# Softmax denominators as an extra column of the output matmuls, and a reordered first pooling pass, in a fused attention and max-out kernel

## The chip, the core and the metric

The kernel runs on one core of a Trainium2 chip. The metric is the device time of one execution in microseconds (us), from a handful of repeated runs. The profile is one further execution, recorded by the hardware profiler.

## What is computed

Two steps follow each other. The first is induced-set attention: 32 learned vectors attend to all tokens of a batch and give `h` (32 x 128), and then each token attends to these 32 rows. The second is a max-out feed-forward layer on the result.

```
B, N, m, C = 4, 12544, 32, 128          # d_ff = 1024
def mab(q, kv):
    s = scale * (q @ kv.T);  s = s - s.max(-1)
    a = exp(s);  a /= a.sum(-1) + 1e-09
    return a @ kv
h = mab(I, x)                            # 32 x 128 per batch
y = mab(x, h)                            # 12544 x 128 per batch
g = maximum(y @ w1, y @ w2)
out = g @ w_out
```

The kernel uses max(a, b) = a + max(0, b - a). With E the exponentials of a token's 32 scores and d their sum, the result is

out = (E @ (h w1 w_out) + relu(E @ (h (w2 - w1))) @ w_out) / d.

The first product is called the linear term here. Its small matrix, 32 x 128 per batch, is `m1`; `hwd` is h (w2 - w1), 32 x 1024. The division by d comes last, so only d is needed per token, at the end.

## The kernel before

**Pooling, batch 0.** The tokens of batch 0 arrive by DMA in eight units: five of 16 blocks of 128 tokens, then 2, 8 and 8 blocks. Per unit, `u_transpose` transposes the blocks on TensorE into PSUM and copies them out, half on VectorE and half on ScalarE. `u_scores` multiplies them with the inducing vectors and takes the exponential on ScalarE. `u_accum` sums exponentials (with a matrix of ones) and the weighted tokens on TensorE. The three are staggered: in the round in which unit i is transposed, unit i-1 is scored and unit i-2 accumulated. `u_h` makes `hT4` from the sums. The weights arrive on the same DMA queue; GpSimd makes three quarters of `w21` = w2 - w1 and VectorE one (line 660).

**Main loop.** A batch has 98 blocks of 128 tokens. They are cut into `Block`s of 16 (batch 0 starts with 2, 4 and 8), and each of these into `Part`s of two 128-column groups. The loop runs over a list `seq` of bursts. A burst (lines 452 to 508) issues row-tiled matmuls into four PSUM banks, 128 x 512 each (line 472), optionally opens two final banks with the linear term ("lead", line 487), and empties the four banks with a relu, each on VectorE (line 503) or ScalarE (line 507). A final (lines 520 to 571) takes 16 matmuls with `woutp` (line 543) into one PSUM bank, VectorE multiplies the 128 x 256 result by the reciprocals (line 559), and after two finals a DMA of 256 KB goes out (line 569), from GpSimd's queue for batches 0 to 2 and from SP's for batch 3. There are 196 bursts and 196 finals. Where no lead was made, the final begins with the linear term itself, from the masked copy `m1d` (line 534).

**Denominators.** `dens` runs once for each of the 30 blocks: one matmul of 4 columns for each 128-column group against `ones4` (line 428), into a PSUM bank of its own, and one reciprocal on VectorE for the whole block (line 437).

**The next batch beside it.** While batch b is in the main loop, batch b+1 is pooled at fixed places of `seq`, given by `at`. `p1_scores` and `p1_accum` run on TensorE; GpSimd adds the exponentials up into `eacc` (128 x 16 x 32, line 317). At place 40 `small_fold` sums the 16 slices of `eacc` with one VectorE reduction (line 322); at 42 `small_h` sums over the partitions with a matrix of ones (line 333) and makes `hT4` (lines 336 and 338); at 43 and 44 `small_hwd` and `small_m1` follow.

**What sets the order.** All engines run a fixed order, written out by the program (`manual_schedule`). A small planner, `Model`, keeps a clock for TensorE, VectorE and ScalarE when the program is built; `bank` gives out the PSUM bank that it thinks comes free first, and `pick` gives each relu to the engine that it thinks ends it first. It charges VectorE for extra work through `ev(..., extra)`.

Of the kernel before, what the change touches and what calls it, by code (L numbers as in the profile page):

```python
# [9 lines left out]
F16 = mybir.dt.float16  # L10
F32 = mybir.dt.float32
AF = mybir.ActivationFunctionType
ALU = mybir.AluOpType
ET = mybir.EngineType

# [36 lines left out]
def kernel(  # L52
# [9 lines left out]
    nc = tc.nc  # L62
    B, N, C = x.shape
    M = inducing.shape[0]
# [5 lines left out]
    P1B = 16  # L70
# [8 lines left out]
    NU = len(units)  # L79
# [76 lines left out]
    with tc.manual_schedule(engines={ET.PE, ET.DVE, ET.Activation, ET.Pool, ET.SP}):  # L156
# [26 lines left out]
        def u_transpose(i):  # L183
            t, g0, n = units[i]
            xn = xn_of(0, t)
            step = 4 if i == NU - 1 else 8
            for g in range(g0, g0 + n, step):
                m = min(step, g0 + n - g)
                bi, ps = bank([128, 8, 128], F16)
                end = 0.0  # L190
                for j in range(m):
                    nc.tensor.transpose(ps[:, j, :], xn[:, g + j, :], identity16)  # L192
                    end = model.pe(0.056)
                k = p1_blocks[t][0] + g
                dst = xT_tiles[0][:, k : k + m, :]
                if (g // step) % 2 == 0:
                    nc.vector.tensor_copy(out=dst, in_=ps[:, 0:m, :])  # L197
                    model.bank_free[bi] = model.ev("DVE", 64 * m, end)
                else:
                    nc.scalar.copy(out=dst, in_=ps[:, 0:m, :])  # L200
                    model.bank_free[bi] = model.ev("ACT", 128 * m, end)
# [118 lines left out]
        def small_fold(b):  # L320
            es = smp.tile([128, 1, M], F32, name=f"esum_{b}", tag="esum")
            nc.vector.reduce_sum(  # L322
                out=es[:, 0, :],
                in_=st[b]["eacc"].rearrange("p k m -> p m k"),
                axis=mybir.AxisListType.X,
            )
            model.ev("DVE", P1B * M, 0.0)
            st[b]["esum"] = es[:, 0, :]
# [36 lines left out]
        m1_tiles = [consts.tile([128, C], F16, name=f"m1_{i}") for i in range(2)]  # L365
        m1d_tiles = [consts.tile([128, 4, C], F16, name=f"m1d_{i}") for i in range(2)]
        ones4 = consts.tile([128, 4], F16, name="ones4")
        mask = consts.tile([128, 4, 1], F16, name="mask")

        def small_m1(b):  # L370
# [6 lines left out]
            nc.scalar.copy(out=m1, in_=ps[:, 0:128])  # L377
            model.bank_free[bi] = model.ev("ACT", 128, end)
            nc.gpsimd.tensor_mul(
                m1d,  # L380
                m1[:, None, :].broadcast_to((128, 4, 128)),
                mask.broadcast_to((128, 4, 128)),
            )
# [3 lines left out]
        class Block:  # L387
# [37 lines left out]
            def dens(self):  # L425
                bi, ps = bank([128, 512])
                for tt in range(self.t):
                    nc.tensor.matmul(  # L428
                        out=ps[:, 4 * tt : 4 * (tt + 1)],
                        lhsT=self.e2[:, 128 * tt : 128 * (tt + 1)],  # L430
                        rhs=ones4,
                        start=True,
                        stop=True,
                    )
                    end = model.pe(0.025, max(model.bank_free[bi], self.ready))
                self.rp = rpp.tile([128, self.t, 4, 1], F32, name=f"rp_{self.name}", tag="rp")
                nc.vector.reciprocal(
                    out=self.rp.rearrange("p t q o -> p (t q o)"), in_=ps[:, 0 : 4 * self.t]
                )
                model.bank_free[bi] = model.ev("DVE", 16, end, 0.1)  # L440

        class Part:
# [9 lines left out]
            def burst(self, u, lead=()):  # L452
# [30 lines left out]
                for s in range(2):  # L483
                    for part, q in lead:
# [3 lines left out]
                            out=part.fin[q][1][:, 128 * s : 128 * (s + 1)],  # L488
                            lhsT=part.blk.e2[r, 128 * tt : 128 * (tt + 1)],
                            rhs=st[part.blk.b]["m1"][r, :],  # L490
# [4 lines left out]
                    if lead:  # L495
                        model.pe(0.056, 0.0, "row")
                for q in range(4):
# [22 lines left out]
            def final(self, i):  # L520
# [10 lines left out]
                for s, (q, tt) in enumerate(cols):  # L531
                    o = ps[:, 128 * s : 128 * (s + 1)]
                    if start:
# [3 lines left out]
                            rhs=st[blk.b]["m1d"][:, q, :],  # L537
# [4 lines left out]
                    for jb in range(NJB):  # L542
                        nc.tensor.matmul(  # L543
                            out=o,
# [10 lines left out]
                if self.tn == 2:  # L555
                    rp = blk.rp[:, self.t0 : self.t0 + 2, i, :]
                else:
                    rp = blk.rp[:, 0, 2 * i : 2 * i + 2, :]
                nc.vector.tensor_mul(  # L559
                    self.osb[:, h : h + 2, :],  # L560
                    ps[:, 0:256].rearrange("p (s c) -> p s c", s=2),
                    rp.broadcast_to((128, 2, 128)),
                )
                model.bank_free[bi] = model.ev("DVE", 256, end)
# [38 lines left out]
        nc.vector.tensor_copy(out=ones4, in_=mask.rearrange("p q o -> p (q o)"))  # L603
# [28 lines left out]

        last = NU - 3
        for i in range(last - 1):
            u_transpose(i)
            if i >= 1:
                u_scores(i - 1)
            if i >= 2:
                u_accum(i - 2)
            keep_warm(1)  # L640

        u_transpose(last - 1)
        u_scores(last - 2)
# [4 lines left out]
        u_accum(last - 3)  # L648
# [3 lines left out]
        for i in range(last - 2, NU):  # L652
            u_accum(i)
# [53 lines left out]
        for g, (p, u) in enumerate(seq):  # L707
# [3 lines left out]
            p.burst(u, lead)  # L711
            for blk in stages.get(g, ()):
                blk.stage()
            if g == 0:
                small_m1(0)
# [3 lines left out]
            if u == 0 and p.t0 == 0:  # L719
                p.blk.dens()  # L720
# [38 lines left out]
```

The softmax here doesn't subtract the row's maximum and nothing guards it: scores larger than these inputs give would overflow.

## Time and profile before

| | |
|---|---|
| median of 6 runs | 342.92 us (342.32 to 343.96) |
| the profiled execution's own time | 342.84 us |
| its span in the profile | 341.1 us |
| granted TensorE clock | 1.0 of full speed |
| TensorE busy | 329.4 us (97%) |
| VectorE busy | 298.2 us (87%) |
| ScalarE busy | 270.1 us (79%) |
| GpSimd busy | 87.0 us (26%) |

PE is TensorE, PEld its weight loads, DVE VectorE, ACT ScalarE, POOL GpSimd; L543 is line 543 of the kernel. A group's busy time counts overlapping instructions of an engine once, and a mean is the time of one from start to end, so the two differ where instructions of one engine overlap. The time in brackets in a timeline line is idle time of the engine just before, with what ended it. The 1.7 us between span and time lie outside the recorded instructions.

### The profile page before, as it was taken

The page shows a single profiled execution, that of the slowest core. Times are in us where ns is not written, and L with a number is a line of the kernel's source. Part 1 is how long each engine was busy: PE and PEld are TensorE (multiplying, and loading weights), DVE is VectorE, ACT ScalarE, POOL GpSimd, SP SyncE. Part 2 cuts the span into 40 slices and gives each one's busy share as a digit, 9 for nine tenths or more (in the row PEclk, how much of TensorE's full clock was granted, in tenths as well). Part 3 has the DMA queues.
Part 4 walks back from the last instruction along what each step waited for, and adds up shares of the span by engine and source line. Part 5 has one row for each costly group of instructions (what it writes and reads, how often), then busy time and mean ns, then how long its engine had stood idle before and what let it go on. Part 6 is the DMA issues. An engine that isn't in the chain of part 4 may idle for free.

```text
span 341.1 us, 14479 instructions
## 1 busy us (share of the span) xinstructions
PE 329.4 (97%) x6346; PEld 263.9 (77%) x6346; DVE 298.2 (87%) x622; ACT 270.1 (79%) x523; POOL 87.0 (26%) x148
## 2 busy tenths in 40 slices
PE   8788999999999999999999999999999999999996
PEld 3685688888868878888877887887877787878875
DVE  2247999999899999999998999999998998989994
ACT  1657988777888877887888877787889888889882
POOL 7243111454422233553222131423212100000000
PEclk9999999999999999999999999999999999999999
DMA  7999699589928984995228992212212222222222
GB/s 135 210 270 214 143 263 232 156 171 216 232 83 162 278 192 108 183 249 156 96 93 165 251 209 88 94 65 94 93 67 94 80 96 92 96 95 94 96 96 108
DMA packets 53423, 50.42 MB, mean 148 GB/s; under 512 B 41456, under 2 KB 42128, under 8 KB 53360
## 3 DMA queue, kind: packets, MB, share of 16 engines
q0 software_dynamic: 11408, 33.43, 36.9%
q1 hardware_dynamic: 41952, 16.08, 21.6%
q8 instruction: 49, 0.80, 0.9%
q14 instruction: 14, 0.11, 0.1%
HBM read 27.28 MB, written 25.69 MB: 155 GB/s over the span
## 4 chain that ended last, share of the span: by engine, by line
PE 85%; DMA 4%; DVE 3%; ACT 3%; POOL 2%; issue 2%; POOLq 0%; DVEq 0%
PE ps L543 55%; PE ps L472 18%; DMA xn<-in_x_dram 4%; PE ps L487 4%; ACT relu L507 2%; PE ps L297 2%; PE ps L275 2%; PE ps L407 2%; DVE relu L503 1%; POOL xn L119 1%; DVE o L559 1%; POOL xn L114 1%; DVE esum L322 1%; PE ps L428 1%; PE ps L534 0%
## 5 line engine op out<-in xcount | busy, mean ns | idle before, releaser
L507 ACT ACTIVATE relu<-ps 128x512 f16<-128x512 f32 x445 | 235.8, 602 | 45.4 <-PE ps L472 33.0
L503 DVE TENSOR_SCALAR relu<-ps 128x512 f16<-128x512 f32 x339 | 218.3, 680 | 5.2 <-PE ps L472 4.1
L543 PE MATMUL ps<-woutp,relu 128*128 128x128 f16 x3136 | 209.1, 220 | 0.0
L543 PEld LDWEIGHTS <-relu 128*128 128x128 f16 x3136 | 176.4, 98 | 30.8 <-issue 21.1
L559 DVE TENSOR_TENSOR o<-ps,rp 128x256 f32<-128x256 f32 x196 | 81.9, 418 | 15.4 <-PE ps L543 12.5
L472 PE MATMUL ps<-e,hwd 32*128 32x256 f16 (+1 forms) x1632 | 83.0, 268 | 1.1 <-DVE relu L503 0.3
L569 POOL DMA_DIRECT2D out_dram<-o x75 | 41.0, 547 | 163.6 <-DVE o L559 111.9
L472 PEld LDWEIGHTS <-hwd 32*128 32x128 f16 x1632 | 27.1, 92 | 20.0 <-issue 4.4
L487 PE MATMUL ps<-m,e 32*128 32x128 f16 x372 | 29.8, 214 | 1.2 <-DVE relu L503 0.5
L487 PEld LDWEIGHTS <-e 32*128 32x128 f16 x372 | 18.4, 92 | 7.5 <-issue 4.4
L317 POOL TENSOR_TENSOR eacc<-eacc,et 128x512 f32<-128x512 f32 (+1 forms) x18 | 18.5, 1028 | 0.3
L284 ACT ACTIVATE et<-ps 128x512 f16<-128x512 f32 (+1 forms) x21 | 11.4, 544 | 4.7 <-PE ps L275 4.7
L417 ACT ACTIVATE e<-ps 128x512 f16<-128x512 f32 (+2 forms) x30 | 14.9, 549 | 0.0
L200 ACT COPY xT<-ps 128x1024 f16<-128x1024 f16 (+1 forms) x6 | 5.6, 941 | 11.3 <-PE ps L192 11.3
L114 POOL DMA_DIRECT2D xn<-in_x_dram x21 | 11.5, 550 | 5.3 <-DMA xn<-in_x_dram 4.7
L197 DVE COPY xT<-ps 128x1024 f16<-128x1024 f16 (+2 forms) x8 | 4.9, 608 | 8.3 <-PE ps L192 8.3
L275 PE MATMUL ps<-inducingT,xT 128*128 128x32 f16 x294 | 10.6, 176 | 0.0
L297 PE MATMUL ps<-et,xn 128*128 128x32 f16 x294 | 10.6, 176 | 0.0
L192 PE MATMUL ps<-identity,xn 128*128 128x128 f16 x98 | 6.7, 219 | 3.1 <-DMA xn<-in_x_dram 2.7
L275 PEld LDWEIGHTS <-xT 128*128 128x128 f16 x294 | 9.6, 96 | 0.0
L297 PEld LDWEIGHTS <-xn 128*128 128x128 f16 x294 | 9.5, 96 | 0.0
L407 PE MATMUL ps<-xT,hT 128*32 128x512 f16 (+2 forms) x120 | 8.7, 349 | 0.6 <-DVE w L660 0.4
(65 smaller groups left out, 112.1 us busy)
## 6 DMA issues: line engine op xcount, KB each, us to landing
out_dram<-o POOLq DMA_DIRECT2D x72, 256.0 KB, 3.2
xn<-in_x_dram POOLq DMA_DIRECT2D x23, 512.0 KB, 9.1
out_dram<-o SPq DMA_DIRECT2D x24, 256.0 KB, 2.0
wf<-in_moe_w_dram POOLq DMA_DIRECT2D x2, 512.0 KB, 14.2
xn<-in_x_dram POOLq DMA_DIRECT2D x2, 256.0 KB, 13.7
out_dram<-o POOLq DMA_DIRECT2D x3, 128.0 KB, 5.4
xT<-xn SPq DMA_TRANSPOSE x21, 6.0
xn<-in_x_dram POOLq DMA_DIRECT2D x4, 64.0 KB, 9.3
```

Source lines behind the costliest of these rows:

```text
L114: nc.gpsimd.dma_start(out=xn_of(b, i)[:, 0:n, :], in_=xr[b, :, k0 : k0 + n, :])
L275: nc.tensor.matmul(out=ps[:, j * M : (j + 1) * M], lhsT=xT_tiles[b % 2][:, k0 + j, :], rhs=inducingT, start=True, stop=True,)
L297: nc.tensor.matmul(out=ps[:, 0:M], lhsT=xn[:, j, :], rhs=et[:, j, :], start=(j == 0), stop=(j == n - 1),)
L317: nc.gpsimd.tensor_add(out=acc, in0=acc, in1=et[:, 0:n, :])
L407: nc.tensor.matmul(out=ps[32 * q : 32 * (q + 1), 0 : self.width], lhsT=st[self.b]["hT4"][:, 32 * q : 32 * (q + 1)], rhs=xT[:, q % self.g], ...
L472: nc.tensor.matmul(out=ps[:, jj * w : (jj + 1) * w], lhsT=st[blk.b]["hwd"][r, 128 * jb : 128 * (jb + 1)], rhs=blk.e2[r, 128 * self.t0 : 12 ...
L487: nc.tensor.matmul(out=part.fin[q][1][:, 128 * s : 128 * (s + 1)], lhsT=part.blk.e2[r, 128 * tt : 128 * (tt + 1)], rhs=st[part.blk.b]["m1" ...
L503: nc.vector.tensor_scalar(out=dst, in0=src, scalar1=0.0, scalar2=None, op0=ALU.max)
L507: nc.scalar.activation(out=dst, in_=src, func=AF.Relu)
L543: nc.tensor.matmul(out=o, lhsT=self.relu[:, jb, q, tt, :], rhs=woutp[:, jb, :], start=False, stop=(s == 1 and jb == NJB - 1),)
L559: nc.vector.tensor_mul(self.osb[:, h : h + 2, :], ps[:, 0:256].rearrange("p (s c) -> p s c", s=2), rp.broadcast_to((128, 2, 128)),)
L569: eng.dma_start(out=outr[blk.b, :, k : k + nst, :], in_=self.osb[:, 0:nst, :])
```

## The change

The tiles of `m1` and `m1d` get 132 columns instead of 128, set to 1 beforehand in `m1` and masked in `m1d`. The linear-term matmuls take 129 of them, so the 129th column of each 128-column group of a final's PSUM bank is the denominator. `dens`, `ones4` and their 100 matmuls and 30 reciprocals are gone. Each of the 196 finals has a reciprocal of its own on VectorE, 2 elements wide, just before its multiplication. The planner charges a final 0.16 us more.

Three more places change. `small_fold` runs on GpSimd, as four additions that halve `eacc` (8, 4, 2 and 1 slices of 32), instead of VectorE's reduction. `small_m1(0)` is moved from after the first burst to between that burst's matmuls and its relus, and `m1d` is made in two halves. In the pooling of batch 0, each round transposes unit i, accumulates unit i-1 and then scores unit i; the last three units' copies all go to VectorE, and the last unit is copied in one piece.

```diff
-            step = 4 if i == NU - 1 else 8
+            step = 8
...
-                if (g // step) % 2 == 0:
+                if i >= NU - 3 or (g // step) % 2 == 0:
                     nc.vector.tensor_copy(out=dst, in_=ps[:, 0:m, :])
...
         def small_fold(b):
-            es = smp.tile([128, 1, M], F32, name=f"esum_{b}", tag="esum")
-            nc.vector.reduce_sum(out=es[:, 0, :], in_=st[b]["eacc"]..., axis=X)
-            model.ev("DVE", P1B * M, 0.0)
-            st[b]["esum"] = es[:, 0, :]
+            acc = st[b]["eacc"]
+            n = P1B // 2
+            while n:
+                nc.gpsimd.tensor_add(out=acc[:, 0:n, :], in0=acc[:, 0:n, :], in1=acc[:, n : 2 * n, :])
+                n //= 2
+            st[b]["esum"] = acc[:, 0, :]
...
-            nc.gpsimd.tensor_mul(m1d, m1[:, None, :]..., mask...)
+            for q in (0, 2):
+                nc.gpsimd.tensor_mul(m1d[:, q : q + 2, :], m1[:, None, :]..., mask[:, q : q + 2, :]...)
...
-            def dens(self):
...
-                            out=part.fin[q][1][:, 128 * s : 128 * (s + 1)],
+                            out=part.fin[q][1][:, MS * s : MS * s + C + 1],
-                            rhs=st[part.blk.b]["m1"][r, :],
+                            rhs=st[part.blk.b]["m1"][r, 0 : C + 1],
...
+                pv = ps[:, 0 : 2 * MS].rearrange("p (s c) -> p s c", s=2)
+                rp = rpp.tile([128, 2, 1], F32, name=f"rp_{self.name}_{i}", tag="rp")
+                nc.vector.reciprocal(out=rp, in_=pv[:, :, C : C + 1])
                 nc.vector.tensor_mul(
                     self.osb[:, h : h + 2, :],
-                    ps[:, 0:256].rearrange("p (s c) -> p s c", s=2),
+                    pv[:, :, 0:C],
                     rp.broadcast_to((128, 2, 128)),
                 )
-                model.bank_free[bi] = model.ev("DVE", 256, end)
+                model.bank_free[bi] = model.ev("DVE", 256, end, 0.16)
...
         for i in range(last - 1):
             u_transpose(i)
             if i >= 1:
-                u_scores(i - 1)
-            if i >= 2:
-                u_accum(i - 2)
+                u_accum(i - 1)
+            u_scores(i)
             keep_warm(1)
-
         u_transpose(last - 1)
-        u_scores(last - 2)
+        u_accum(last - 2)
         u_transpose(last)
         u_transpose(last + 1)
         u_scores(last - 1)
         u_transpose(last + 2)
-        u_accum(last - 3)
+        u_accum(last - 1)
         u_scores(last)
         u_scores(last + 1)
         u_scores(last + 2)
-        for i in range(last - 2, NU):
+        for i in range(last, NU):
             u_accum(i)
...
-            p.burst(u, lead)
+            p.burst(u, lead, (lambda: small_m1(0)) if g == 0 else None)
...
-            if g == 0:
-                small_m1(0)
...
-            if u == 0 and p.t0 == 0:
-                p.blk.dens()
```

The order of the changed program differs in one more way, which the diff does not show: with the new charge the planner gives VectorE 305 relus and ScalarE 479, where it gave them 339 and 445.

## The prediction

> **What bounds it now.** I read the chain that ended last first, then the groups by shape, then the engines' busy time in stretches that I cut at the stages, then timelines. Chain and groups:
>
> ```profile
> PE 85%; DMA 4%; DVE 3%; ACT 3%; POOL 2%; issue 2%; POOLq 0%; DVEq 0%
> ```
>
> ```profile
> L428 PE MATMUL ps<-ones,e 128*128 128x4 f16 x100 | 6.8, 165 | 0.0
> L437 DVE RECIPROCAL rp<-ps 128x16 f32<-128x16 f32 x23 | 5.7, 247 | 0.0
> L437 DVE RECIPROCAL rp<-ps 128x4 f32<-128x4 f32 x6 | 1.0, 172 | 0.0
> L317 POOL TENSOR_TENSOR eacc<-eacc,et 128x512 f32<-128x512 f32 x15 | 17.6, 1170 | 0.2
> L317 POOL TENSOR_TENSOR eacc<-eacc,et 128x64 f32<-128x64 f32 x3 | 0.9, 317 | 0.0
> ```
>
> TensorE sets the end, but VectorE runs close behind it. The stretches (length, then busy us of PE, PEld, DVE, ACT, POOL) show how close:
>
> ```profile
> 38.00:96.00 58.00, 57.43 (x1166) 47.58 (x1168) 55.40 (x116) 46.31 (x89) 20.13 (x33) 1.00 0.86 195
> 168.00:190.00 22.00, 21.61 (x396) 16.86 (x388) 20.39 (x42) 19.42 (x41) 4.95 (x10) 1.00 0.60 141
> 246.00:269.00 23.00, 22.62 (x416) 17.56 (x414) 20.97 (x44) 20.43 (x43) 5.30 (x10) 1.00 0.21 83
> 269.00:334.00 65.00, 64.63 (x1212) 51.66 (x1210) 60.81 (x122) 56.92 (x112) 0.54 (x1) 1.00 0.25 94
> ```
>
> So each added VectorE us must find a place in 2 to 7% of idle time, while every TensorE us removed counts where VectorE leaves room. VectorE's true prices are its start-to-start times, in the timeline at the turn from batch 0 to 1:
>
> ```profile
> 92.97 0.32 POOL L317 TENSOR_TENSOR eacc<-eacc,et 128x64 f32<-128x64 f32 x1
> ...
> 93.32 1.04 DVE L322 TENSOR_REDUCE esum<-eacc 128x32 f32<-128x512 f32 x1 [1.10 <-POOL eacc L317]
> ...
> 94.27 0.68 DVE L503 TENSOR_SCALAR relu<-ps 128x512 f16<-128x512 f32 x1
> ...
> 94.87 0.42 DVE L559 TENSOR_TENSOR o<-ps,rp 128x256 f32<-128x256 f32 x1
> ...
> 95.20 0.68 DVE L503 TENSOR_SCALAR relu<-ps 128x512 f16<-128x512 f32 x1
> ...
> 96.13 0.35 DVE L336 RECIPROCAL hrec<-ps 128x32 f32<-128x32 f32 x1
> ...
> 96.51 0.29 DVE L338 TENSOR_TENSOR hT<-hacc,hrec 128x128 f16<-128x128 f32 x1
> ```
>
> A relu holds VectorE for 0.60 us (94.27 to 94.87), a final's multiplication for 0.33 (94.87 to 95.20): successors start before the end. But the multiplication at 96.51, which needs the reciprocal's result, starts 0.38 after it, 0.03 after its end.
>
> **The reciprocals.** Each final gains one, with its multiplication waiting for it on the same engine. By width, 247 ns for 16 columns and 172 for 4 give 6.25 ns a column, so 160 ns for 2; with the 0.03 wait, 0.19 us a final, 196 x 0.19 = 37.2 us. Bounds: 0.09 us (the start-to-start time of a 4-column reciprocal before an independent relu) to 0.38 (the row at 96.13); I take 0.19, since form and dependence are those of that row and only the width is less. Behind the waiting multiplication are queued the next burst's relus, and behind those TensorE's next PSUM banks. Removed from VectorE: 30 block reciprocals at 0.09 to 0.16 (4.6 us), three reductions at 0.87 start to start (2.6), and 339 - 305 = 34 relus at 0.60 (20.4). Net +9.6 us. ScalarE takes the 34 relus at 0.49 (eight in a row last 4.03 us at 169.6; 16.7 us); it has 71 us idle in the span, and this work lies beside TensorE.
>
> [...]
>
> **The matmuls of the denominators.** From a final's first weight load to the next burst's, 4 denominator matmuls between them add little:
>
> ```profile
> 37.95 0.90 PEld L543 LDWEIGHTS <-relu 128*128 128x128 f16 x16
> ...
> 38.81 0.20 PEld L428 LDWEIGHTS <-e 128*128 128x128 f16 x4
> ...
> 39.03 0.12 PEld L472 LDWEIGHTS <-hwd 32*128 32x128 f16 x8
> ...
> 101.86 0.90 PEld L543 LDWEIGHTS <-relu 128*128 128x128 f16 x16 [0.41 <-issue]
> ...
> 102.86 0.23 PEld L472 LDWEIGHTS <-hwd 32*128 32x128 f16 x16
> ```
>
> 1.08 us against 1.00: 0.08 for each of 23 blocks, 1.9 us in all (the small blocks add under 0.1). One PSUM bank more is free meanwhile, which I price at nothing: these stretches show TensorE 98 to 100% busy, so banks are not what it waits for. The 129th column is 1/128 of 392 matmuls that stream 128 columns; at the 63 ns that one of the finals' 16 takes (1.00/16), 392 x 63/128 = 0.2 us; at the least nothing, if weight loads hide it. I take 0.1.
>
> In the stretches 38-96, 112-168 and 190-246, 13 blocks lie; VectorE loses 10, 9 and 10 relus there against 35 or 36 finals, so its load stays within 0.6 us of before. There TensorE's gain is real: 13 x 0.08 = **-1.0**. In the last batch (269-334) I count 44 finals, 72 relus before and 67 after. VectorE's slots go from 72 x 0.60 + 44 x 0.33 + 5 x 0.16 = 58.5 to 67 x 0.60 + 44 x 0.52 = 63.1 us, against 65.0 - 5 x 0.08 = 64.6 that TensorE needs. VectorE would be 98% full in fixed order, and it now loses 4.2 us there idle, mostly waiting for a final's last matmul. I let 0.8 us of stalls reach TensorE: **+0.4** net (0 stalls: -0.4; all of the idle kept: 63.1 + 4.2 = 67.3, so +2.3).
>
> **The fold.** Before, VectorE stood 1.10 us for GpSimd and then 0.95 in the reduction. The finals' starts show what reached TensorE: 93.37 to 96.47 is 3.10 us where a final with lead takes 1.44 and `small_h` 0.35, so 1.3 lost; in the turns at 171 and 249, 1.92 for 1.44, so 0.5 each. After: four GpSimd additions of 256, 128, 64 and 32 elements; the two L317 rows give 0.20 us + 1.9 ns an element, so 0.68, 0.44, 0.32 and 0.26, with gaps of about 0.08 (the setup's GpSimd operations) 2.0 us. In batch 0 it starts when the addition at 92.97 ends and is ready at 95.3, while TensorE wants it at 94.5, where line 333's matmuls start now: 0.8 stall, 0.5 gained. In the others the last `eacc` addition is three places earlier; only GpSimd's output DMA, which waits for a multiplication, stands before the fold (170.19 to 170.75 at batch 1). Ready at 172.8, wanted at 173.4. These turns are VectorE-bound after the change (20 relus remain 20), so I count half of the 0.5s. Sum **-1.0** (bounds -2.3, if the fold is never waited for, to +0.5, if GpSimd's queue makes each turn wait).
>
> **The start.** The first final stands behind `m1d`:
>
> ```profile
> 28.66 1.03 POOL L379 TENSOR_TENSOR m1d<-m,mask 128x512 f16<-128x512 f16 x1 [1.64 <-ACT m L377]
> 29.75 0.22 PE L534 MATMUL ps<-m1d,e 128*128 128x128 f16 x1 [1.18 <-POOL m1d L379]
> ```
>
> With `m1` copied ahead of the first relus and `m1d` in halves (half of 1.03 or a little more), the first half is there before TensorE gets to it: the 1.18 goes. Next is late what the copy delays, two ScalarE relus by its 0.29, and the first finals' multiplications, whose end frees banks for the next burst here, two reciprocals at 0.19. Pooling: a round now waits for the ScalarE copy (1.01 us) of its own unit, so it lasts 1.0 transposes + 1.1 copy's end + 0.3 second half of the scores + 0.2 warming = 2.6 us; four rounds from 7.3 reach 17.8, where the data of the fifth unit came at 17.5. So 0.3 is lost there, but after the last data at 20.2 one accumulation (0.6) less is left. I take 0.35 gained (bounds: 0.6 gained, if the rounds cost nothing; 1.0 lost, if each takes a third of a us longer than worked out). Start: -1.18 - 0.35 + 0.29 + 0.38 = **-0.85**. At the tail one reciprocal lies before the last multiplication: **+0.2**.
>
> **Sum.** -1.0 + 0.4 - 1.0 - 0.85 + 0.1 + 0.2 = -2.15, on the profiled execution's own 342.84 (span 341.1 and 1.74 around it; 0.08 under the median): 340.7 us.
>
> **Rivals.**
> 1. VectorE becomes the bound (slower). In the start, turns and last batch (27-38, 96-112, 168-190, 246-269, 269-334) lie 85 finals: 85 x 0.19 = 16.2, less 6 relus (3.6), 16 block reciprocals (2.6) and 2 reductions (1.7), so +8.3 us. The idle time there is 1.8 + 1.2 + 1.6 + 2.0 + 4.2 = 10.8. If a third of it can be used, 4.7 reach the end; with the gains outside (1.0, batch 0's turn 0.5, the start 0.85) and +0.3: 345.5. It decides when under 60% of that idle time is usable. For it: fixed order, 94% full already. Against: 38-96 ran 96% full with TensorE 99% busy.
> 2. Everything fits (faster still): reciprocals hidden, all 1.9 of the denominators, 2.3 of the folds and 1.5 at the start: 342.84 - 5.7 + 0.3 = 337.4. Against: the slots of the last batch.
> 3. No change: the pooling order costs 1.0 instead of -0.35, and GpSimd's fold stalls TensorE as long as the reduction did (0 instead of -1.0): 340.7 + 2.35 = 343.0.
>
> **How the numbers follow.** My forecast has 0.45, rival 1 0.25, rival 2 0.13, rival 3 0.17. About 0.3% (1 us) is what a measurement of this kernel can tell from no change. Faster takes my forecast, rival 2 and a little of rival 3: 0.60; same 0.15; slower 0.25. The range runs from near rival 2's end to just short of rival 1's: 338.0 to 345.2.
>
> **What would show it.** Right: L428 and L437's 16-column rows gone with nothing new on the chain in 38-96; a 2-column reciprocal near 160 ns with its multiplication 0.19 after its start; no L534 wait at 28; DVE 97% or more busy in the last batch with TensorE spacing near 1.33 and 1.44; a wait of L333 for GpSimd near 0.8 at the first turn only. Wrong: finals in the last batch spaced well over 1.45 on average with waits on VectorE's relus, or a first burst later than 26.6.

## The result, and the profile after

The changed kernel takes 345.73 us (median of 21 executions, 344.21 to 347.83) against 343.52 for the kernel before beside it: ratio 1.0066 [1.0053, 1.0078]. It is slower by 2.2 us, where a gain of 2.15 was forecast, and lies 0.5 us above the top of the range. The profiled execution took 345.81 us, span 344.0; before it was 342.84 and 341.1.

Each execution's mean granted TensorE clock is on record too. It is 0.998 or more in some and 0.993 to 0.995 in most others, and this goes with 1.0 us: the kernel before, over all that follows, has a median of 342.93 us in 37 executions at 0.998 or more and of 343.92 in 51 at 0.993 to 0.995. The last section shows what goes with it in the profiles. The versions have the two in different shares, so beside the medians of all executions I give differences "at full clock": a version's executions at 0.998 or more, against those of the kernel before beside them. The changed kernel is slower by 1.7 us at full clock (344.64, 11 executions) and by 2.0 at the lower one.

I read the same views in the same order. First the chain that ended last, from the page of the changed kernel:

```profile
PE 78%; DMA 6%; issue 6%; ACT 4%; POOL 3%; DVE 2%; POOLq 0%
```

TensorE lost seven points of the chain. "issue", time in which an engine waits for nothing that the profile shows, rose from 2 to 6%; that entry becomes important below. The groups by shape show the new operations as forecast:

```profile
L543 DVE RECIPROCAL rp<-ps 128x2 f32<-128x2 f32 x196 | 32.1, 164 | 10.3 <-PE ps L529 7.8
...
L326 POOL TENSOR_TENSOR eacc<-eacc 128x256 f32<-128x256 f32 x3 | 2.2, 734 | 0.1
L326 POOL TENSOR_TENSOR eacc<-eacc 128x128 f32<-128x128 f32 x3 | 1.4, 453 | 0.2
```

A reciprocal takes 164 ns (160 forecast). The busy time by stretches (length, then busy us of PE, PEld, DVE, ACT, POOL):

```profile
38.00:96.00 58.00, 55.82 (x1116) 45.03 (x1112) 53.29 (x133) 49.11 (x96) 21.58 (x36) 1.00 0.92 195
112.00:168.00 56.00, 55.52 (x1113) 44.67 (x1111) 52.30 (x130) 48.97 (x95) 19.53 (x31) 1.00 0.92 190
168.00:190.00 22.00, 21.70 (x389) 16.59 (x387) 20.88 (x54) 19.96 (x40) 7.32 (x15) 1.00 0.50 122
190.00:246.00 56.00, 55.74 (x1117) 44.76 (x1118) 52.66 (x131) 49.07 (x97) 16.27 (x24) 1.00 0.54 126
246.00:269.00 23.00, 22.69 (x408) 17.30 (x406) 21.87 (x55) 20.47 (x41) 7.14 (x14) 1.00 0.24 89
269.00:337.00 68.00, 67.77 (x1231) 53.54 (x1232) 65.66 (x165) 60.43 (x119) 1.08 (x2) 1.00 0.25 92
```

Only the first row shows a clear loss: TensorE is 96% busy in 38 to 96 where it was 99%. In the other rows it is 99% busy or more, within 1% of before, and yet the same finals take longer, so this view hides part of the loss. The start and the first turn, from the timeline:

```profile
27.71 1.23 POOL L380 TENSOR_TENSOR m1d<-m,mask 128x264 f16<-128x264 f16 x2
...
28.42 0.22 PE L520 MATMUL ps<-m1d,e 128*128 128x129 f16 x1 [0.18 <-POOL m1d L380]
...
94.07 0.42 DVE L544 TENSOR_TENSOR o<-ps,rp 128x256 f32<-128x256 f32 x1
...
94.29 1.98 POOL L326 TENSOR_TENSOR eacc<-eacc 128x256 f32<-128x256 f32 x4
...
96.33 0.41 PE L333 MATMUL ps<-eacc,ones 128*128 128x32 f32 x2 [1.17 <-POOL eacc L326]
```

The wait for `m1d` is 0.18 us instead of 1.18, and the first final starts at 28.47 instead of 29.81. At the first turn TensorE waits 1.17 us for GpSimd's fold; in the other two turns it does not wait.

Where the time went, from the starts of the finals in the two timelines (us, after minus before): up to the first final -1.33; batch 0 (final 1 to 50) +2.14; batch 1 (50 to 99) +0.59; batch 2 (99 to 148) +0.30; batch 3 (148 to 196) +0.73; from the last final to the end of the span +0.54. The sum is +2.97.

What ended TensorE's waits in the loop (the waits view, PE, 36 to 340 us; total, times, longest), for the changed kernel:

```profile
PE ps L333 <- POOL eacc L326: 1.2, 1, 1.2
PE ps L471 <- issue: 1.1, 1, 1.1
PE ps L471 <- DVE relu L489: 0.5, 3, 0.2
PE ps L456 <- issue: 0.5, 1, 0.5
PE ps L471 <- ACT e L418: 0.4, 2, 0.2
PE ps L471 <- ACT relu L493: 0.3, 1, 0.3
```

and the kernel before:

```profile
PE ps L487 <- DVE relu L503: 0.5, 2, 0.3
PE ps L472 <- DVE relu L503: 0.3, 1, 0.3
```

Two waits for the fold and for "issue" stand out, and the lead matmuls (L471) wait more. This view has only a part of it: "issue" apart, it lists 1.2 us at the lead matmuls of the changed kernel and 0.5 at those of the kernel before, while the starts of these matmuls give 2.5 us more (third row below). So I added up the time from each TensorE matmul's start to the next one's start, by kind of step, from the 4th to the 193rd final (my own sum over the trace's records):

| us | before | changed | changed, 2nd profile |
|---|---|---|---|
| whole stretch | 295.91 | 299.62 | 299.10 |
| steps round the denominators, with the turn to the next burst | 22.83 | 20.78 | 20.77 |
| steps within the groups of four lead matmuls, without the next row's | 10.78 | 13.31 | 13.89 |
| stalls without a releaser | 0 | 2.02 | 1.12 |
| final to `small_h` | 0.40 | 1.50 | 1.50 |

The denominators' removal brings its 2.0 us. It is eaten by the leads (+2.5 to 3.1), the stalls without a releaser (+1.1 to 2.0) and the first fold (+1.1). The experiments ask what each of these is.

### The profile page after: what moved, and what is told of

Its sections match the earlier page's. It is cut to its first block, busy times and chain, and to the rows that moved or that the text cites. A ratio compares the mean times of both kernels' runs of the same rounds, so it can differ in the third digit from the quotient of the medians.

```text
span 344.0 us, 14447 instructions
## 1 busy us (share of the span) xinstructions
PE 331.0 (96%) x6246; PEld 260.2 (76%) x6246; DVE 303.3 (88%) x752; ACT 284.6 (83%) x556; POOL 93.2 (27%) x164
## 3 DMA queue, kind: packets, MB, share of 16 engines
q0 software_dynamic: 11408, 33.43, 38.2%
## 4 chain that ended last, share of the span: by engine, by line
PE 78%; DMA 6%; issue 6%; ACT 4%; POOL 3%; DVE 2%; POOLq 0%
PE ps L529 50%; PE ps L456 17%; PE ps L471 4%; DMA wf<-in_moe_w_dram 4%; ACT relu L493 3%; DMA xn<-in_x_dram 2%; PE ps L277 2%; PE ps L299 2%; PE ps L408 2%; DVE relu L489 1%; POOL out_dram L554 1%; POOL xn L116 1%; DVE o L544 1%; ACT e L418 1%; POOL eacc L319 0%
## 5 line engine op out<-in xcount | busy, mean ns | idle before, releaser
L493 ACT ACTIVATE relu<-ps 128x512 f16<-128x512 f32 x479 | 251.5, 606 | 33.4 <-PE ps L456 25.0
L489 DVE TENSOR_SCALAR relu<-ps 128x512 f16<-128x512 f32 x305 | 198.5, 682 | 2.5 <-PE ps L456 1.7
L544 DVE TENSOR_TENSOR o<-ps,rp 128x256 f32<-128x256 f32 x196 | 83.2, 425 | 6.8
L543 DVE RECIPROCAL rp<-ps 128x2 f32<-128x2 f32 x196 | 32.1, 164 | 10.3 <-PE ps L529 7.8
L471 PE MATMUL ps<-m,e 32*128 32x129 f16 x372 | 32.3, 216 | 2.8 <-issue 1.1
L471 PEld LDWEIGHTS <-e 32*128 32x128 f16 x372 | 18.9, 92 | 10.0 <-issue 4.5
L199 DVE COPY xT<-ps 128x1024 f16<-128x1024 f16 (+1 forms) x8 | 5.1, 637 | 8.4 <-PE ps L194 8.4
L202 ACT COPY xT<-ps 128x1024 f16<-128x1024 f16 x5 | 5.1, 1012 | 8.5 <-PE ps L194 8.5
## 6 DMA issues: line engine op xcount, KB each, us to landing
xn<-in_x_dram POOLq DMA_DIRECT2D x2, 256.0 KB, 13.3
```

The lines of the kernel that those rows point to most:

```text
L471: nc.tensor.matmul(out=part.fin[q][1][:, MS * s : MS * s + C + 1], lhsT=part.blk.e2[r, 128 * tt : 128 * (tt + 1)], rhs=st[part.blk.b]["m1" ...
L489: nc.vector.tensor_scalar(out=dst, in0=src, scalar1=0.0, scalar2=None, op0=ALU.max)
L493: nc.scalar.activation(out=dst, in_=src, func=AF.Relu)
L543: nc.vector.reciprocal(out=rp, in_=pv[:, :, C : C + 1])
L544: nc.vector.tensor_mul(self.osb[:, h : h + 2, :], pv[:, :, 0:C], rp.broadcast_to((128, 2, 128)),)
```

## The experiments

### Which part of the change costs

`start_only` is the kernel before with the three edits of the start (pooling order, copies, `small_m1` and the two halves of `m1d`).

```diff
+            u_scores(i)
...
+            p.burst(u, lead, (lambda: small_m1(0)) if g == 0 else None)
```

> Before, with the three changes at the start alone: the new pooling order of batch 0, small_m1(0) ahead of the first relus, m1d in two halves. Theory A (the start gains, the main loop loses): the first final starts 1.3 us earlier, as in the changed kernel, nothing else moves, so 1.0 to 1.5 us faster than before. Rival (the start's gain is given back later, because the next batch's loads set the pace): under 0.4 us faster.

Measured: 341.75 us, ratio 0.9949 [0.9929, 0.9969]: 1.75 us gained, but 0.97 at full clock, which all five of its executions have and only 4 of 16 of the kernel before beside them.

`fold_only` is the kernel before with the fold on GpSimd.

```diff
-            nc.vector.reduce_sum(...)
+            while n:
+                nc.gpsimd.tensor_add(out=acc[:, 0:n, :], in0=acc[:, 0:n, :], in1=acc[:, n : 2 * n, :])
```

> Before, with the fold of eacc on GpSimd alone. Theory A: the three turns no longer lose the 1.3 and twice 0.5 us to VectorE's reduction, but at the first turn TensorE waits about 1.1 us for GpSimd before line 333's matmuls, so 0.5 to 1.5 us faster than before. Rival (the fold on GpSimd is what made the changed kernel slower): 0.5 to 2 us slower.

Measured: 342.51, 0.9966 [0.995, 0.9983]: 1.2 us gained, 0.74 at full clock.

`col_only` is the kernel before with the column, the reciprocals and the planner's charge.

```diff
-            def dens(self):
...
+                nc.vector.reciprocal(out=rp, in_=pv[:, :, C : C + 1])
```

> Before, with the denominators as a 129th column and a reciprocal for each final alone (with the planner's charge); old pooling order, old fold, old place of small_m1. Theory A: this part holds all of the loss. TensorE is rid of 2.1 us of denominator matmuls and waits more than that before the second lead matmul of a final pair, for a bank that ScalarE's third relu of the burst before still empties: 2 to 4.5 us slower than before. Rival (fold or stalls without a named wait made the loss): within 1 us of before.

Measured: 348.72, 1.0156 [1.0135, 1.0178]: 5.4 us lost. It has no execution at full clock; at 0.993 to 0.995 it is 4.9 us slower than the kernel before (348.69 and 343.76). `after_reduce` is the changed kernel with VectorE's reduction put back.

```diff
-                nc.gpsimd.tensor_add(out=acc[:, 0:n, :], in0=acc[:, 0:n, :], in1=acc[:, n : 2 * n, :])
+            nc.vector.reduce_sum(...)
```

> The changed kernel with VectorE's single reduction in place of GpSimd's fold. Theory A: the turns lose what the reduction costs, so 0.5 to 1.5 us slower than the changed kernel (about 3.5 us slower than before). Rival (the fold on GpSimd is what made it slower): 0.5 to 2 us faster than the changed kernel.

Measured: 347.59, 1.0116 [1.0082, 1.015], so the fold gains in the changed kernel too (1.3 us at full clock, 345.98 against 344.64). By the medians the three parts add, -0.51 - 0.34 + 1.56 = +0.71% against 0.66 measured, but that is luck: at equal clock they are -0.97 - 0.74 + 4.9 = +3.2 us, where 1.7 to 2.0 were measured. The column is the only part that loses; how much depends on what stands beside it.

`start_fold` is the change without the column.

> Before, with the three changes at the start and the fold on GpSimd, without the column. If the parts add up, 0.9949 x 0.9966 = 0.9915 of before, about 2.9 us faster; if the fold's gain needs the old start, no more than start_only's 0.5%.

Measured: 341.80, 0.9934 [0.9908, 0.996]: 2.3 us gained of the 2.9 expected. At full clock it is 1.6 (two executions), and there the two parts add (0.97 + 0.74). From here to the changed kernel the column costs 3.3 us at full clock.

### What in the column costs

`after_128` leaves the 129th column out of the matmuls.

```diff
-                            rhs=st[part.blk.b]["m1"][r, 0 : C + 1],
+                            rhs=st[part.blk.b]["m1"][r, 0:C],
```

> The changed kernel with the linear-term matmuls 128 columns wide again (the 129th column is left out, the reciprocals take the last of the 128, so the values are others; every instruction and the order stay). Theory A (the lead matmuls wait for PSUM banks): within 0.5 us of the changed kernel. Rival C (the odd width of 129 columns makes the row-tiled matmuls slower, 93 leads at 0.04 to 0.08 us): 4 to 7 us faster than the changed kernel.

Measured: 345.38, 1.0043 [1.0017, 1.007]. The interval overlaps that of the changed kernel, so the width costs at most about 1 us; at full clock the two are 0.25 us apart (344.39 and 344.64). The profiles show nothing of it: where no bank is late, the starts within a group of leads are 2 to 4, 53 and 3 ns apart at both widths.

`after_norecip` leaves the reciprocals out, in the same order of the relus.

```diff
-                nc.vector.reciprocal(out=rp, in_=pv[:, :, C : C + 1])
+                rp = ones32[:, 0:2].rearrange("p (s o) -> p s o", o=1)
```

> The changed kernel with the 196 reciprocals left out (the multiplications take ones, so the division is left out); the order and the split of the relus, 305 and 479, stay. Theory A1 (what VectorE spends on reciprocals and on waiting for them holds up the banks): 3 to 5 us faster than the changed kernel, about 341 to 342 us. Theory A2 (the planner's new split, three relus of a burst on ScalarE ahead of a lead, holds up the banks): under 1 us faster, the second lead matmul still waits about 0.1 us.

Measured: 342.18, 0.995 [0.9928, 0.9971]. The reciprocals cost 1.16%, some 4 us, and 3.0 at full clock (344.64 to 341.64). `after_nodep` keeps all 196 and only lets the multiplication read ones, so that the division is left out.

```diff
-                    rp.broadcast_to((128, 2, 128)),
+                    ones32[:, 0:2].rearrange("p (s o) -> p s o", o=1).broadcast_to((128, 2, 128)),
```

> The changed kernel with its 196 reciprocals in place, but the multiplications take ones instead of their results, so that none waits for a reciprocal on its own engine (the division is left out). Order and split stay. If the wait counts (0.19 us a final with it, 0.08 to 0.10 without), about half of what leaving the reciprocals out gained comes back: 1.5 to 2.5 us faster than the changed kernel. If a wait between chained VectorE operations costs nothing, no change; if only the wait counts, the whole 3.9 us.

Measured: 342.23, 0.996 [0.9934, 0.9985], the same as without the reciprocals. So 196 more operations on VectorE cost nothing that can be measured here; making the next operation wait for each costs 3.5 us, or 3.0 at full clock, where the ranges lie well apart (341.31 to 342.32 in six executions, 344.21 to 345.82 in the changed kernel's eleven). Its trace was taken once more:

> One profile of the kernel whose multiplications take ones instead of the reciprocals' results, for the waits of its lead matmuls. If the dependent wait makes the leads wait, their sum falls from 9.6 us to about that of the kernel without reciprocals, 6.8; if the time came back elsewhere, it stays near 9.6.

The same final of the last batch in the timeline of the changed kernel

```profile
316.39 1.07 PE L529 MATMUL ps<-woutp,relu 128*128 128x128 f16 x16
316.43 0.16 DVE L543 RECIPROCAL rp<-ps 128x2 f32<-128x2 f32 x1
...
316.63 0.42 DVE L544 TENSOR_TENSOR o<-ps,rp 128x256 f32<-128x256 f32 x1
316.97 0.68 DVE L489 TENSOR_SCALAR relu<-ps 128x512 f16<-128x512 f32 x1
...
317.62 0.35 PE L471 MATMUL ps<-m,e 32*128 32x129 f16 x4
...
317.90 0.51 PE L529 MATMUL ps<-woutp,relu 128*128 128x128 f16 x6
```

and of `after_nodep_look`:

```profile
314.10 0.16 DVE L543 RECIPROCAL rp<-ps 128x2 f32<-128x2 f32 x1
314.16 1.07 PE L529 MATMUL ps<-woutp,relu 128*128 128x128 f16 x16
314.18 0.40 DVE L544 TENSOR_TENSOR o<-ps,ones 128x256 f32<-128x256 f32 x1
...
314.50 0.68 DVE L489 TENSOR_SCALAR relu<-ps 128x512 f16<-128x512 f32 x1
...
315.39 0.29 PE L471 MATMUL ps<-m,e 32*128 32x129 f16 x4
...
315.61 0.56 PE L529 MATMUL ps<-woutp,relu 128*128 128x128 f16 x7
```

From the reciprocal to the relu behind the multiplication it is 0.54 us against 0.40. The four leads then take 0.28 us (317.62 to 317.90) against 0.22, and the next final starts 1.51 us after this one instead of 1.45. The waits that go with the dependence are 60 to 110 ns long, but for one of 33. In the last batch, from the 148th to the 196th final, the independent version takes 67.74 us against 68.73. Over the loop the leads' row falls from 13.3 to 11.9 and the stalls without a releaser from 2.02 to 0.18. So nearly half of the difference is in the leads. More than half is in those stalls, which the last group of runs is about; that the dependence brings them is not shown, and a second profile of the changed kernel has 1.12 us of them beside 13.89 us in the leads.

Is it VectorE's standing still, or the later release of the final's bank? `after_split` puts a relu between the two operations.

```diff
+                    if eng == "DVE" or q == 3:
+                        while pending:
+                            pending.pop(0)()
...
+                pending.append(rest)
```

> The changed kernel with the final's multiplication taken away from its reciprocal: it is issued behind the first relu of the next burst that goes to VectorE (or ahead of the fourth bank's), so that VectorE does independent work while the reciprocal ends. The price is that the final's PSUM bank is held about 0.6 us longer. Theory A (VectorE standing at the dependent multiplication costs the time): the changed kernel's 345.7 less 1 to 3 us, ratio 0.998 to 1.004. Theory B (what counts is how soon the final's bank comes free): slower than the changed kernel, 347 to 350, ratio 1.01 to 1.02. The planner's split moves to 241 and 543, which is a change beside the one meant and may cost ScalarE time.

Measured: 348.25, 1.0145 [1.0118, 1.0171]. It decides little: the planner, seeing the bank held longer, moved 64 more relus to ScalarE (89% busy, 83% in the changed kernel). The run leaves the question open. For the leads the traces answer it. The second lead matmul opens the second final bank; where it starts more than 10 ns behind the first, I looked up what released it:

| released by | before | `start_fold` | changed | `after_nodep_look` | `after_norecip` |
|---|---|---|---|---|---|
| a relu on VectorE | 8 | 5 | 15 | 3 | 3 |
| a relu on ScalarE | 13 | 15 | 27 | 27 | 27 |
| a final's multiplication | 3 | 2 | 0 | 0 | 0 |
| another operation | 4 | 4 | 8 | 6 | 6 |
| all, of 93 | 28 | 26 | 50 | 36 | 36 |

Without the dependence, 12 waits for VectorE's relus are gone. No lead of the changed kernel waits for a final's multiplication, so what reaches the leads is the relus queued behind the multiplication, not the later release of the final's bank. The waits for ScalarE's relus come with the relus that moved there, and stay.

### The planner's prices

`after_charge0` takes the planner's charge for a reciprocal away, so that VectorE keeps 338 relus.

```diff
-                model.bank_free[bi] = model.ev("DVE", 256, end, 0.16)
+                model.bank_free[bi] = model.ev("DVE", 256, end)
```

> The changed kernel with the planner's charge of 0.16 us for a final taken back, so that the split is nearly that of before (338 and 446 relus), with the reciprocals. Theory A1: VectorE has 34 relus more and is over its time, so 3 us or more slower than the changed kernel. Theory A2: 2 us or more faster than the changed kernel.

Measured: 354.64, 1.0317 [1.0289, 1.0345]. Here VectorE does not take the reciprocals beside its old relus without a further loss (345.73 with 305 relus). But moving 34 relus to ScalarE has a price too: `after_norecip` has neither denominators nor reciprocals and still only equals `start_fold` (342.18 and 341.80), though 2.0 us of TensorE work are gone. Its leads' row is 11.8 against 9.9.

`after_cal` gives the planner measured prices.

```diff
-        return extra + (... else 0.045 + n / 1200.0)
+        return extra + (... else 0.045 + n / 1130.0)
...
-                model.bank_free[bi] = model.ev("DVE", 256, end, 0.16)
+                model.bank_free[bi] = model.ev("DVE", 256, end, 0.2)
```

> The changed kernel with the planner told the measured prices: 0.20 us more for a final instead of 0.16, and a ScalarE relu of 0.50 us instead of 0.47. If the waits before the leads come from a plan that is off by these few hundredths, 1 to 3 us faster than the changed kernel. If they come from the work itself, within 1 us.

Measured: 344.42, 1.0024 [1.0003, 1.0044], with 310 and 474 relus. By the medians that is 1.4 us less loss, for prices that were wrong by 0.04 us a final and 6% of a ScalarE relu's streaming time. But nine of its ten executions are at full clock, and there the loss is 1.2 us instead of 1.7: the better prices bring 0.5 us at most. That may also belong to the stalls of the last group, of which its profile has only one of 0.35 us.

### The fold's wait at the first turn

`start_fold_h` is `start_fold` with `small_h` and what follows it one place later for batch 1's attention.

```diff
+            d = 1 if b == 0 else 0
-            for s, f in ((40, small_fold), (42, small_h), (43, small_hwd), (44, small_m1)):
+            for s, f in ((40, small_fold), (42 + d, small_h), (43 + d, small_hwd), (44 + d, small_m1)):
```

> start_fold with small_h, small_hwd and small_m1 of the first turn one place later, so that GpSimd's fold has a final's time more. The 1.06 us that TensorE waits before line 333's matmuls at the first turn should go: 0.7 to 1.1 us faster than start_fold, about 0.988 of before. Rival (the later hT4 delays batch 1's first bursts by as much): same as start_fold.

Measured: 338.90, 0.9862 [0.9833, 0.989], the lowest median of all versions and faster than both kernels, by 4.2 us than the one before at full clock. That is 2.9 us under `start_fold`, and 2.4 at full clock (two executions of `start_fold`). The profile of `start_fold` shows 1.0 us of waiting for the fold and 0.45 of a stall at TensorE's instruction 3265 that are gone here; the other 0.9 I cannot assign. Its timeline at the turn shows the fold ending before TensorE comes to it, with no wait, and its chain is TensorE's nearly alone:

```profile
91.57 1.99 POOL L324 TENSOR_TENSOR eacc<-eacc 128x256 f32<-128x256 f32 x4
...
93.91 0.36 PE L331 MATMUL ps<-eacc,ones 128*128 128x32 f32 x2
```

```profile
PE 94%; ACT 3%; DVE 2%; issue 0%; DVEq 0%
```

`start_fold_h_cal` adds the planner's better ScalarE price to it.

> start_fold_h with the planner's ScalarE relu at 0.50 us instead of 0.47 (VectorE gets 352 relus instead of 339). If a better price shortens the waits before the leads (4.8 us in start_fold's profile), 0.5 to 1.5 us faster than start_fold_h; if VectorE is then over its time, slower.

Measured: 339.63, 0.988 [0.9842, 0.9917], no gain over the former; at full clock the two are the same (338.75 in two executions, and 338.90). Without the reciprocals the planner's old price does no harm. `after_h_cal` is `after_cal` with the later `small_h`:

> The changed kernel with the first turn's small_h, small_hwd and small_m1 one place later, and the planner given the measured prices (0.20 us for a reciprocal, ScalarE's relu at n/1130). If the parts add: the calibrated version's 344.4 less the 1.4 us wait of line 333, 343.0, ratio 0.998 to 0.999. If the later small_h only moves the stall, as 344.4, ratio 1.002. Whichever, it stays over the version with the start, the fold and the later small_h without the column (338.9).

Measured: 343.32, 1.0007 [0.9984, 1.003]. The turn's wait is gone (0.17 us from final to `small_h` instead of 1.50); the interval still overlaps that of `after_cal`. At full clock it has two executions, 342.65 and 342.81, against 344.38.

### The stalls without a releaser

The changed kernel's timeline of TensorE, and the DMA view of the time before it (72.0 to 76.9 us, then 76.9 to 78.0; the queue lines give packets, MB and the share of the 16 engines, the issue lines KB each and us to landing):

```profile
78.00 0.33 PE L471 MATMUL ps<-m,e 32*128 32x129 f16 x3
79.47 0.21 PE L471 MATMUL ps<-m,e 32*128 32x129 f16 x1 [1.15 <-issue]
```

```profile
q0 software_dynamic: 261, 0.90, 99.3%
issues: line engine op xcount, KB each, median us to landing
xn<-in_x_dram POOLq DMA_DIRECT2D x2, 512.0 KB, 9.4
```

```profile
q8 instruction: 1, 0.02, 5.4%
```

Three of the four lead matmuls ran, and the fourth stood still in the middle of the group, with "issue" as its reason. I counted TensorE's records (matmuls, weight loads and a few of its sequencer) up to each such stall. In the changed kernel they come at number 2753 (79.5 us) and 5571 (153.4), in other versions at 2241, 2753, 3009, 3265, 4290 and 5569: each is 193 to 195 more than a multiple of 256 (once, in `after_charge0`, 189; some records are missing from a trace). Each ends 1.2 to 1.7 us (once 2.1) after the end of a 16 KB packet of the instruction queue q8. There are 49 such packets for 12,500 of TensorE's records, which is 255 records a packet. The packet that ended just before a stall's end is always the n-th where the stalled instruction lies behind the n-th multiple of 256. In 19 traces every n-th packet starts between 0.8 us before and 5.0 us after TensorE crosses the number that lies 256 ahead of the place where such a stall comes. Here it crossed number 2497 at 72.2 us, between the 512 KB loads issued at 69.4 and 72.4; from 72.0 to 76.9 us queue q0 took 99.3% of the DMA engines' time, and the packet started at 77.0. Before the change the same crossing lay at 72.3, the loads at 70.4 and 73.6, the packet started at 74.3, and there was no stall.

`after_shift` adds 66 instructions to TensorE's queue at the very start, in place of some of the warming matmuls that run before any data is there.

```diff
-                nc.tensor.matmul(out=ps, lhsT=warm[:, 0:128], rhs=warm, start=True, stop=True)
+                n = 4 if j < split else 1
+                for p in range(n):
+                    nc.tensor.matmul(out=ps[:, c * p : c * (p + 1)], ..., rhs=warm[:, 0:c], ...)
```

> The changed kernel with 11 of the 18 warming matmuls at the very start, before any data is there, cut into four of a quarter of the columns: 66 more instructions in TensorE's queue, nothing else. In the profiles so far the stalls of TensorE that have no releaser come at every 256th instruction of its queue (numbers 2241, 2753, 3265, 4289 and 5569, all 193 more than a multiple of 256) and end 1.3 to 1.5 us after a 16 KB packet of the instruction queue that started late, while the loads of the next batch fill the DMA engines. Theory F (TensorE had run out of fetched instructions): the crossing that asks for the late packet, at 72.2 us, comes about 1.5 us earlier against the 512 KB loads at 69.4 and 72.4; the 1.4 us stall at 79.5 goes or shrinks under 0.5, any stall that is left again lies at 193 over a multiple of 256, now 66 instructions earlier in the program; time 1 to 2 us under the changed kernel, ratio 0.999 to 1.004. Theory S (the stalls are scatter and cost nothing in the median): ratio 1.005 to 1.008, as the changed kernel.

Beside it ran the changed kernel as it is:

> The changed kernel as it is, beside the shifted one on the same chip, with a second profile. Both theories: ratio 1.005 to 1.008. Theory F: a stall again at TensorE instruction 2753, near 79.5 us; theory S: stalls at other places.

and the shift in `after_h_cal`, whose profile had a stall of 1.40 us at number 2753:

> The calibrated version with the later small_h and the same 66 instructions at the start; its profile had a stall of 1.40 us at instruction 2753. Theory F: 1 to 1.4 us faster than that version's 343.3, ratio 0.996 to 0.998. Theory S: 1.000 to 1.001. Both: still over the version without the column (338.9).

Measured: the changed kernel again 345.89, 1.0072 [1.0044, 1.01], with stalls again at 2753 (78.7 us, a step of 0.56) and 4290 (121.3, 0.67). `after_shift` 344.96, 1.0038 [1.0019, 1.0058], 1.1 us over the kernel before at full clock (2.0 for the changed kernel beside it), with no stall of this kind in the loop; the leads at that place run through:

```profile
79.54 0.36 PE L480 MATMUL ps<-m,e 32*128 32x129 f16 x4
```

`after_h_cal_shift` 341.48, 0.9934 [0.9916, 0.9952], against 1.0007 [0.9984, 1.003] without the shift: 1.8 us from 66 instructions that compute nothing that is used. All six of its executions are at full clock, though, and only two of twelve without the shift; against these two (342.73) it gains 1.2 us. Its chain of waits:

```profile
PE 91%; DVE 5%; ACT 2%; issue 1%; DVEq 0%
```

So the stalls go with packets that start late and with the places of TensorE's instructions in its queue. That TensorE had run out of instructions is my reading; no record shows it by itself. The stalls are a real part of the loss: 0.6 to 0.9 us in the changed kernel (344.00 at full clock, against 344.64 and, beside it, 344.90), where the intervals of all executions still overlap, and 1.2 in the calibrated one, close to its one profiled stall of 1.4. The other 0.6 us of the 1.8 go with the clock; why the shares of the clock differ is not known.

## Why the prediction was wrong

**The step that failed** is the price of the column in the stretches of batches 0 to 2: "One PSUM bank more is free meanwhile, which I price at nothing: these stretches show TensorE 98 to 100% busy, so banks are not what it waits for", and from it "There TensorE's gain is real: 13 x 0.08 = -1.0". The column's terms were -1.0 + 0.4 + 0.1 + 0.2 = -0.3; `col_only` measured +5.4 us (4.9 at equal clock), and beside the other two parts the column costs 3.3. The matmuls that go bring the 2.0 us that were worked out. But TensorE does wait for banks at the second lead matmul, the new waits being about 0.1 us each, and the busy share hardly shows them: TensorE is still 99% busy in 112 to 168 and in 190 to 246 us, where late second leads have gone from 5 to 11 each. The starts' differences of the leads would have shown 28 such waits in 93 leads before the change; after it there are 50.

**VectorE's time.** The price of 0.19 us was right (0.20 on average from reciprocal to multiplication, 0.08 where the multiplication doesn't need it). What I took from it was wrong: "its load stays within 0.6 us of before" counts the load and not the order. The wait for the result delays the relus behind it (0.54 us from a reciprocal to the relu behind its multiplication, 0.40 without the wait), and these hold the banks (15 of the late second leads, 3 without it). Taking away that dependence alone brought 3.5 us of 345.7 (3.0 at full clock), and the 196 operations without it cost nothing that was measured (342.23 us with them, 342.18 without). "2 to 7% of idle time" was a misreading as well: the rows shown with it leave VectorE 4 to 9% idle (55.40 of 58.00 us busy, 20.97 of 23.00), which did not help it.

**The relus moved to ScalarE** were said to lie beside TensorE. They lengthened the leads by 1.9 us (`start_fold` to `after_norecip`), which is all that the removed matmuls gave.

**The last batch** (+0.4, bounds -0.4 to 2.3) took 0.73 more, of which about 1.0 is the dependence. That term holds, with VectorE at 65.66 of 68.00 us, 97% busy as foretold.

**The start** (-0.85): -1.33 in the profile up to the first final, -1.75 in `start_only` by the medians and -0.97 at full clock. The wait for `m1d` went as said. That the sum comes near is luck: the pooling order gained nothing up to the first burst (26.69 us against 26.63, where 0.35 was counted), and what I charged for late copies and reciprocals, 0.29 + 0.38, was not seen.

**The fold** (-1.0): -1.2 in `fold_only` (-0.7 at full clock), and 1.3 between `after_reduce` and the changed kernel at full clock. The fold lasts 1.98 us as worked out (2.0). The wait at the first turn was 1.17 us instead of 0.8: TensorE is there 0.87 us after the fold's start (96.33 - 1.17 - 94.29), where I had counted 1.2 (93.3 to 94.5) from the order before. No other turn waits, as said.

**The stalls without a releaser** were in no term and no rival. **Rival 1** gave 345.5 and 345.73 was measured, but its mechanism is not what happened. It put the loss in the start, the turns and the last batch, where the start gained and the last batch lost 0.73; the largest loss, 2.14 us, lies in batch 0, with 1.3 us of these stalls and 1.1 of the wait for the first fold. The idle time of VectorE that the rival weighed is not the measure; what stands behind each wait is.

## What to carry to other kernels

A busy share near 100% does not say that an engine waits for nothing (here TensorE was 99% busy from 112 to 168 us, with 11 late second leads): add up the start-to-start steps of one kind of group and compare them with the shortest that occur. Price a small operation that is put before a dependent one by what is queued behind both on that engine and whose buffers those hold, not by its duration: the waits for 196 reciprocals of 0.16 us cost 3.5 us here, the reciprocals without these waits nothing that was measured. A stall with no releaser, at a place in a group where nothing can be late, went here with a late packet of the instruction queue (1.15 us, ended at 79.47, after a packet from 77.0 to 78.0): look for such packets in the DMA records, and try a few dummy instructions ahead. Before pricing a microsecond, compare executions of the same granted clock: 1.0 us lay between the two clocks in the kernel before.

## What I had not expected of the hardware

Beside the 33.43 MB of q0, the instruction queue q8 moved 49 packets of 16 KB in the changed kernel's profile, one for 255 of TensorE's records. With loads of 512 KB in flight a packet started up to 5.0 us after the crossing that preceded it (0.2 to 3.1 in the kernel before, over the same stretch), and TensorE stood for 0.2 to 1.4 us. What asks for a packet was not measured by itself; the counts and the shift are all there is. In the changed kernel's profile no such stall goes with 47 of the 49 packets; with the two others go 2.0 us.

Some profiled executions, of versions with and without the column, have one stretch of 3.4 us in which half of the clock is granted, early in the loop. It is the 0.88 in this row of the stretches of `after_shift`:

```profile
36.00:50.00 14.00, 13.72 (x232) 10.94 (x227) 12.18 (x30) 10.97 (x22) 1.79 (x4) 0.88 0.78 177
```

The changed kernel's profile shows it at full clock:

```profile
36.00:50.00 14.00, 13.72 (x257) 10.97 (x256) 13.39 (x33) 12.31 (x25) 2.33 (x5) 1.00 0.87 191
```

TensorE is busy for 13.72 us in both and does 25 matmuls less in the first. Busy time alone does not show that either. Neither profile of the changed kernel has the stretch, so it is no part of the loss that they show. All nine profiles with a mean clock of 0.993 to 0.995 have one such stretch, beginning between 27.8 and 38.8 us, and none of the ten with 0.998 or more has one. Over a span of 344 us, 3.4 us at half clock would lower the mean by 0.005, my estimate; that the executions that were only timed had such a stretch too where their clock is 0.993 to 0.995 is not shown. The lower clock goes with 1.0 us in the kernel before, 342.93 against 343.92. What brings it is not known.
